# Integer shift adds on 64-bit words, norms' roots on ScalarE, and GpSimd's arithmetic moved to VectorE

## The chip, the cores and the metric

The kernel runs on one core of a Trainium2 chip. The metric is the device time of one execution in microseconds. Five engines work side by side, each with its own in-order queue: TensorE (PE, with its weight loads shown apart as PEld), VectorE (DVE), ScalarE (ACT), GpSimd (POOL) and SyncE (SP), which here only issues DMAs.

## The reference

Two layers, each an attention block A with one key and value head shared by 32 query heads, and a block B that mixes neighbouring rows and runs an MLP. Every block has a layer norm ahead of it, and B has two more inside. Sequence 2048, width 512, head width 16, bf16.

```python
def _A_ref(x, wq, wk, wv, wo):
    q = (x @ wq).reshape(B, S, H, Dh).transpose(0, 2, 1, 3)      # H = 32, Dh = 16
    k, v = x @ wk, x @ wv
    p = _softmax(jnp.einsum("bhqd,bkd->bhqk", q, k) * (Dh ** -0.5))
    o = jnp.einsum("bhqk,bkd->bhqd", p, v)
    return o.transpose(0, 2, 1, 3).reshape(B, S, H * Dh) @ wo
def _B_ref(x, w1, w2, w3, w4):
    h = _gelu(_layernorm(x) @ w1)
    ...                                  # four quarters of h shifted by 1, -1, 2, -2 rows
    x1 = x + hs @ w2
    return x1 + _gelu(_layernorm(x1) @ w3) @ w4        # w3: 512 x 1792
for _ in range(2):
    x = x + _A_ref(_layernorm(x), ...)
    x = x + _B_ref(_layernorm(x), ...)
```

The heavy part is the exponentials: 32 heads x 2048 x 2048 scores in each of two layers.

## The kernel before

A planner in the code (`Plan`) simulates the five engines with a duration for every operation, takes the ready operation with the lowest priority number on each engine, and so writes out a fixed order for each engine's queue, with semaphore waits between them. A table of rules (`MOODS`), chosen anew every 5 us of planned time by a string (`TEMPER`), steers its choices: how many fillers, how eagerly pairs are handed to VectorE, how many shift adds go to GpSimd. The order on the chip is therefore static; when an operation takes another time than planned, the queues wait but do not reorder.

Attention runs over the chunks of queries (four of 512 rows in layer 0; three of 512 and two of 256 in layer 1), in a chunk over 8 blocks of four heads, and in a block over the keys. Its work comes in *halves*: a 128 x 1024 piece of scores, two heads. The 2048 halves are shared out between two ways of taking the exponential.

- A *unit* (`declare_unit`): TensorE writes the scores to two PSUM banks, ScalarE's Exp takes both to EA in bf16 (L1240), TensorE multiplies with the values VP (L1352, four matmuls).
- A *pair* (`declare_pair`): VectorE casts a linear function of the scores to uint16 (L1260, two casts), so that the integer's bits, read as bf16, are a coarse exponential. Two more such rows follow by adding STEP = 43 to the integers, one after the other (`shift_op`, L1297, on GpSimd or VectorE; mostly two rows in one instruction, one of the second step and one of the first). TensorE multiplies all three with values that are weighted by three constants, VD (L1352, twelve matmuls), and their sum is the finer exponential. Five slots J hold pairs under way. `borrow` and `lent` move a waiting add between the two engines.

Beside the attention of one chunk, the planner places the side work of the chunk before it: the output projection, `mixer_in` (norm, norm of the norm, W1, Gelu), `mix` (W2 on shifted rows), `mlp` (norm, W3, Gelu, W4) and the next layer's norm and projections. The last chunk's side work has no attention beside it: the tail. Exp and Gelu are in different tables of ScalarE, so Gelus are bundled, with a table load before and behind.

A norm is `stats` on VectorE (L904, L906), `rstd` for the root, and `apply` on VectorE (L941). In `rstd`, GpSimd adds epsilon (L926, on VectorE at the start) and raises to the power -0.5 with the constant tile MH (L924). `mixer_in` needs the norm of a norm: three small operations more (L930 to L934), a second power, and the scaling of Y to ZR on GpSimd (L1627). In `mlp`, GpSimd also adds Y to X (L1723); in `scale_pair` it spreads reciprocals (L1452), and it copies edge columns of GP (L1673, L1675). A matmul filler (L790, ONES and NIL) keeps TensorE busy when the planner sees it idle.

Of the kernel before, what the change touches and what calls it, by code (L numbers as in the profile page):

```python
# [8 lines left out]
dt = mybir.dt  # L9
# [34 lines left out]
class Plan:  # L44
# [184 lines left out]
    def _pick(self, eng, t, dense=False):  # L229
# [20 lines left out]
        for o in h:  # L250
            if o.ready > t + 1e-9 or o.entry > t + self.EAGER:
                continue
            if eng == "ACT" and self.lock is not None and o.grp is not self.lock:
                continue
            if eng == "ACT" and self.closing and o.side and not all(u.placed for u in self.units[-4:]):
# [36 lines left out]
            best = (key, o)  # L292
            bank = k
# [333 lines left out]

def t_x2(n):
    return 0.066 + n * 0.522e-3
# [10 lines left out]
EPS = 1e-5  # L640
LOG2E = 1.4426950408889634


class Kernel:
# [21 lines left out]
    PORTION = 2  # L666
    QUICK = -1
# [32 lines left out]
        "40600c804b0c70477ac77e7194dc79a6b4c9e70863c1123547ccaa20177534ca0aa0dc405814470c4705413104"  # L700
        "7c1600071c825488640d166cc06053e94164c76c007310602612d80c0c1121b4db0561c3763ca8c50f5820c114"
        "076cc327266480d100a70d6e5394770058ec0700210e43c02c7a1a7307cb2ed6658250706076c138a756cb5e43"
        "813a0801110213220"
    )

    def __init__(self, nc, ins, out):
        self.stretch = -1
        self.nc = nc
        self.ins = ins
        self.out = out  # L710
        self.pl = Plan(nc, self.POOL_BANKS)
# [18 lines left out]
    def memory(self):  # L730
# [40 lines left out]
        self.MH = sb("MH", [2, 16], dt.float32)  # L771
# [52 lines left out]
    def head(self):  # L824
# [24 lines left out]
        fill("POOL", self.MH, -0.5, [("MH",)], 0.1, -8)  # L849
# [15 lines left out]
        def clear(ap, n, tags, prio):  # L865
            op("ACT", lambda e: e.memzero(ap), writes=tags, dur=0.1 + n / 2400, prio=prio)
# [5 lines left out]
        for c in range(4):  # L872
# [7 lines left out]
        fill("POOL", self.SELC, 0.0, [("SELC",)], 0.1, 3)  # L880
# [4 lines left out]
           reads=[("SELC",)], writes=[("SELC",)], dur=0.2, prio=3)  # L885
# [14 lines left out]

    def stats(self, src, tiles, tagf, prio):
# [7 lines left out]
    def rstd(self, tiles, prio, both=False):  # L909
# [3 lines left out]
        k = 2 if both else 1  # L913
        early = prio is not None
        prio = prio if early else self.QUICK
# [3 lines left out]
        var, aux = self.SM[:, 2, a:b], self.SM[:, 3, a:b]  # L919
        one, two = self.SM[:, 0, a:b], self.SM[:, 1, a:b]  # L920
        eng = "DVE" if early else "POOL"

        def power(out, src, tags, r):
            op("POOL", lambda e: e.tensor_tensor(out=out, in0=src, in1=self.MH[:, 0, a:b], op=ALU.pow),  # L924
               reads=tags + [("MH",)], writes=tg(r), dur=0.3 + 0.2 * (b - a), prio=prio)
        op(eng, lambda e: e.tensor_scalar(out=var, in0=mv, scalar1=EPS, scalar2=None, op0=ALU.add),  # L926
           reads=tg("MV"), writes=tg("S2"), dur=0.23 if eng == "POOL" else 0.08, prio=prio, port=True)
        power(one, var, tg("S2"), "R1")
        if both:
            op(eng, lambda e: e.tensor_tensor(out=aux, in0=one, in1=one, op=ALU.mult),  # L930
               reads=tg("R1"), writes=tg("S3"), dur=0.23 if eng == "POOL" else 0.08, prio=prio, port=True)
            op(eng, lambda e: e.tensor_tensor(out=aux, in0=aux, in1=mv, op=ALU.mult),
               reads=tg("MV"), writes=tg("S3"), dur=0.23 if eng == "POOL" else 0.08, prio=prio, port=True)
            op(eng, lambda e: e.tensor_scalar(out=aux, in0=aux, scalar1=EPS, scalar2=None, op0=ALU.add),  # L934
               writes=tg("S3"), dur=0.23 if eng == "POOL" else 0.08, prio=prio, port=True)
            power(two, aux, tg("S3"), "R2")


    def apply(self, out, src, tb, tags, writes, dur, prio):

        self.pl.op("DVE", lambda e: e.tensor_scalar(  # L941
            out=out, in0=src, scalar1=self.MV[:, tb, 0:1], scalar2=self.SM[:, 0, tb:tb + 1],
            op0=ALU.subtract, op1=ALU.mult),
            reads=tags + [("MV", tb), ("R1", tb)], writes=writes, dur=dur, prio=prio, port=True)
# [280 lines left out]
    def declare_unit(self, g):  # L1225
# [14 lines left out]
        o = q.feeds = op("ACT", lambda e: e.activation(self.EA[:, ea, :, :],  # L1240
# [52 lines left out]
    def shift_op(self, d, f, rows):  # L1293
# [3 lines left out]
        o = self.pl.op(eng, lambda e: e.tensor_scalar(  # L1297
            out=self.J[:, d, :], in0=self.J[:, f, :], scalar1=float(self.STEP), scalar2=1.0, op0=ALU.add, op1=ALU.mult),
            reads=[t for r in rows for t in self.jtag(r - 1)], writes=[t for r in rows for t in self.jtag(r)],
            dur=t_x4(1024 * n) if eng == "DVE" else 0.264 + 0.859 * n, prio=2, side=False, port=True,  # L1300
# [316 lines left out]
    def mixer_in(self, la, c, tiles, tail):  # L1617
# [4 lines left out]
        for part in self.portions(tiles):  # L1622
            self.stats(lambda tb: self.X[:, tb, :], part, lambda tb: ("X", tb), None)
            self.rstd(part, None, both=True)
            for tb in part:
                self.apply(self.Y[:, tb % 6, :], self.X[:, tb, :], tb, [("X", tb)], [("Y", tb % 6)], 0.33, None)
                op("POOL", lambda e, tb=tb: e.tensor_scalar(  # L1627
                    out=self.ZR[:, tb % 4, :], in0=self.Y[:, tb % 6, :], scalar1=self.SM[:, 1, tb:tb + 1],
                    scalar2=0.0, op0=ALU.mult, op1=ALU.add),
                   reads=[("Y", tb % 6), ("R2", tb)], writes=[("ZR", tb % 4)],  # L1630
                   dur=0.68, prio=self.QUICK, port=True)
# [5 lines left out]
        for f in range(4):  # L1637
# [10 lines left out]
            if tail:  # L1648
                op("ACT", lambda e, f=f, L=L: e.activation(self.GP[:, par, f, 2:2 + n],
# [10 lines left out]
        if not tail:  # L1660
            grp = Group()
            op("ACT", lambda e: e.activation(self.GP[:, par, :, 2:2 + n], self.GP[:, par, :, 2:2 + n],  # L1662
# [46 lines left out]
    def mlp(self, la, tiles, tail):  # L1709
# [12 lines left out]
        for tb in tiles:  # L1722
            op("POOL", lambda e, tb=tb: e.tensor_tensor(out=self.X[:, tb, :], in0=self.Y[:, tb % 6, :],  # L1723
                                                       in1=self.X[:, tb, :], op=ALU.add),
               reads=[("Y", tb % 6)], writes=[("X", tb)], dur=1.24, port=True)
        for f in range(14):
# [10 lines left out]
            if tail:  # L1737
                op("ACT", lambda e, f=f, L=L: e.activation(self.G2E[f][0][:, 0:n], self.PB[:, L.bank, 0:n],
# [14 lines left out]
    def gelus(self, tiles, joined=(), grp=None):  # L1753

        grp = grp or Group()
        for i in range(len(tiles)):
            self.pl.op("ACT", lambda e, i=i: e.activation(  # L1757
# [65 lines left out]
```

## Time and profile before

| | us |
|---|---|
| three runs, median (lowest to highest) | 1448.71 (1447.62 to 1449.34) |
| span of the profiled execution | 1444.3 |
| PE busy | 1418.6 (98%) |
| ACT busy | 1374.8 (95%) |
| DVE busy | 1321.9 (92%) |
| POOL busy | 1175.3 (81%) |

The span runs from the first to the last instruction of one profiled execution; the times of the runs also hold what lies around it, about 4.4 us at the median. Busy time is the union of an engine's instructions; consecutive ones overlap, so a group's mean is longer than its busy time over its count. Matmul ends are modelled, so a busy PE isn't PE at its peak. A row of the groups gives line, engine, operation, output and input with shapes, count, busy us, mean ns of one, and the idle time in front of them with what ended it.

### The profile page before, as it was taken

What the parts mean: (1) busy time and instruction counts of PE and PEld (TensorE: products, weight loads), DVE (VectorE), ACT (ScalarE), POOL (GpSimd) and SP (SyncE); (2) the same over time, 40 slices, a digit from 0 to 9 for tenths busy, and PEclk for the clock granted to TensorE, in tenths of its full rate; (3) what the DMA queues carried; (4) which work ended last, traced back from release to release, by engine and by line L of the source; (5) the groups of instructions that cost most, each with busy time, mean ns of one, the idle gap of its engine ahead of it and who ended that gap; (6) DMA issues with size and microseconds to landing.
All of it is one profiled execution on the core that took longest, in us unless ns stands there. A gap on an engine that the chain in (4) does not pass through costs nothing.

```text
span 1444.3 us, 65460 instructions
## 1 busy us (share of the span) xinstructions
PE 1418.6 (98%) x29768; PEld 637.7 (44%) x29768; DVE 1321.9 (92%) x2392; ACT 1374.8 (95%) x1463; POOL 1175.3 (81%) x846
## 2 busy tenths in 40 slices
PE   8999999999999999999999999999999999999999
PEld 4344334443444444444454444434434445545555
DVE  8999999999999999999988899999998999979863
ACT  7999999999999999999979999999999999999952
POOL 3888899998988978988855788998887988888841
DMA  6100100001000000010000000100000000000000
GB/s 221 31 5 6 21 6 6 5 6 20 6 5 7 6 7 4 7 21 3 2 3 3 3 11 9 21 6 5 6 12 17 6 6 14 8 17 12 7 14 25
DMA packets 32662, 21.76 MB, mean 15 GB/s; under 512 B 13056, under 2 KB 31872, under 8 KB 32384
## 3 DMA queue, kind: packets, MB, share of 16 engines
q1 hardware_dynamic: 32384, 17.57, 5.3%
q8 instruction: 233, 3.82, 1.1%
q14 instruction: 45, 0.37, 0.1%
HBM read 7.90 MB, written 2.10 MB: 7 GB/s over the span
## 4 chain that ended last, share of the span: by engine, by line
ACT 57%; PE 26%; DVE 8%; POOL 7%; issue 1%; DMA 0%; SPq 0%; POOLq 0%
ACT EA L1240 54%; PE PB L1197 8%; PE PB L1352 8%; PE PB L790 8%; POOL J L1297 6%; DVE J L1260 4%; ACT G L1757 2%; DVE J L1297 1%; PE PB L1121 1%; DVE ST L904 1%; PE PB L988 1%; POOL SM L924 1%; ACT L1240 1%; ACT GP L1662 1%; DVE G L1742 0%
## 5 line engine op out<-in xcount | busy, mean ns | idle before, releaser
L1240 ACT ACTIVATE EA<-PB 128x1024 bf16<-128x1024 f32 x1381 | 1272.0, 1149 | 11.3 <-PE PB L1197 10.6
L1297 POOL TENSOR_SCALAR J<-J 128x2048 uint16<-128x2048 uint16 (+1 forms) x550 | 1003.2, 1824 | 165.7 <-DVE J L1260 75.8
L1260 DVE TENSOR_SCALAR J<-PB 128x512 uint16<-128x512 f32 x1334 | 853.9, 680 | 49.9 <-PE PB L1197 44.5
L1197 PE MATMUL PB<-QT,KT 32*128 32x512 bf16 (+1 forms) x4608 | 586.5, 359 | 7.6 <-ACT EA L1240 3.1
L1352 PE MATMUL PB<-J,VD 128*32 128x256 bf16 (+1 forms) x8988 | 423.1, 264 | 6.5 <-DVE J L1297 1.4
L1352 PE MATMUL PB<-EA,VP 128*32 128x256 bf16 (+1 forms) x6220 | 351.9, 264 | 3.2 <-ACT EA L1240 1.8
L1197 PEld LDWEIGHTS PB<-QT,KT 32*128 32x128 bf16 x4608 | 159.6, 91 | 366.7 <-ACT EA L1240 277.8
L1352 PEld LDWEIGHTS PB<-J,VD 128*32 128x32 bf16 x8988 | 191.0, 95 | 154.4 <-issue 103.0
L1352 PEld LDWEIGHTS PB<-EA,VP 128*32 128x32 bf16 x6220 | 144.7, 95 | 142.0 <-issue 120.9
L790 PE MATMUL PB<-ZT,W 128*32 128x512 bf16 (+2 forms) x2816 | 169.5, 342 | 0.0
L1297 DVE TENSOR_SCALAR J<-J 128x2048 uint16<-128x2048 uint16 (+1 forms) x155 | 110.5, 713 | 13.0 <-POOL J L1297 10.9
L790 PE MATMUL PB<-W,G 128*32 128x512 bf16 x1624 | 105.6, 381 | 0.4 <-issue 0.4
L790 PEld LDWEIGHTS PB<-ZT,W 128*32 128x32 bf16 x2816 | 63.3, 96 | 34.4 <-issue 25.8
L1742 DVE CAST G<-PB 128x512 bf16<-128x512 f32 (+2 forms) x126 | 71.4, 577 | 4.7 <-PE PB L790 4.2
L924 POOL TENSOR_TENSOR SM<-SM,MH 128x2 f32<-128x2 f32 (+1 forms) x69 | 53.3, 774 | 21.8 <-DVE SM L926 13.3
L1757 ACT ACTIVATE G<-G 128x1792 bf16<-128x1792 bf16 x29 | 46.9, 1683 | 23.6 <-DVE G L1742 23.6
L790 PEld LDWEIGHTS PB<-W,G 128*32 128x32 bf16 x1624 | 36.8, 96 | 40.1 <-issue 15.3
L1723 POOL TENSOR_TENSOR X<-Y,X 128x512 bf16<-128x512 bf16 x32 | 39.4, 1242 | 12.2 <-DVE Y L1705 10.1
L904 DVE BATCH_NORM_STATS2 ST<-X 128x6 f32<-128x512 bf16 x64 | 42.8, 679 | 2.2 <-DMA X<-in_A_x_dram 1.8
L1392 DVE CAST ACCF<-PB 128x512 bf16<-128x512 f32 (+1 forms) x65 | 39.9, 614 | 0.8 <-PE PB L1352 0.7
L790 PE MATMUL PB<-WO,OT 128*32 128x512 bf16 x512 | 37.6, 381 | 0.0
L790 PE MATMUL PB<-W,GP 128*32 128x512 bf16 x512 | 34.2, 380 | 1.0 <-ACT GP L1662 1.0
(106 smaller groups left out, 706.2 us busy)
## 6 DMA issues: line engine op xcount, KB each, us to landing
OT<-ACCF SPq DMA_DIRECT2D x432, 8.0 KB, 1.8
W<-in_B_w_dram SPq DMA_DIRECT2D x2, 1792.0 KB, 13.9
X<-in_A_x_dram SPq DMA_DIRECT2D x8, 256.0 KB, 6.0
QT<-QS SPq DMA_DIRECT2D x32, 64.0 KB, 2.5
out_dram<-OUTB SPq DMA_DIRECT2D x16, 128.0 KB, 1.7
OT<-ACCF SPq DMA_DIRECT2D x112, 4.0 KB, 2.2
W<-in_B_w_dram SPq DMA_DIRECT2D x2, 512.0 KB, 8.6
WQ<-in_A_wq_dram SPq DMA_DIRECT2D x1, 512.0 KB, 5.5
```

The lines of the kernel that those rows point to most:

```text
L790: ins = e.matmul(self.PB[32 * g:32 * g + 32, bank, 0:n], lhsT=lhsT[:, 32 * g:32 * g + 32], rhs=rhs, start=start, stop=stop, tile_position= ...
L904: op("DVE", lambda e, tb=tb: e.bn_stats(self.ST6[:, tb, :], src(tb)), reads=[tagf(tb)], writes=[("ST", tb)], dur=0.606, prio=prio)
L924: op("POOL", lambda e: e.tensor_tensor(out=out, in0=src, in1=self.MH[:, 0, a:b], op=ALU.pow), reads=tags + [("MH",)], writes=tg(r), dur=0. ...
L1197: ins = e.matmul(self.PB[:, bank, j * n:(j + 1) * n], lhsT=self.KT[32 * h:32 * h + 32, la, (kb + j) * 128:(kb + j + 1) * 128], rhs=self.QT ...
L1240: o = q.feeds = op("ACT", lambda e: e.activation(self.EA[:, ea, :, :], self.PB[:, L.bank[0]:L.bank[0] + 2, :], ACTF.Exp, scale=0.25), writ ...
L1260: o = op("DVE", lambda e, i=i, L=L: e.tensor_scalar(out=self.J[:, 3 * s, i * 512:(i + 1) * 512], in0=self.PB[:, L.bank, :], scalar1=128 * ...
L1297: o = self.pl.op(eng, lambda e: e.tensor_scalar(out=self.J[:, d, :], in0=self.J[:, f, :], scalar1=float(self.STEP), scalar2=1.0, op0=ALU.a ...
L1352: ins = e.matmul(self.PB[32 * x:32 * x + 32, A.bank, p * hw:p * hw + hw], lhsT=v[:, la, kb + j, :], rhs=ap[:, i, j * w + u * hw:j * w + u ...
L1392: self.last_copy = op("DVE", lambda e: e.tensor_copy(acc, self.PB[:, A.bank, 0:n]), writes=[ac] + am, dur=t_ps(n), prio=0, side=False, give=A)
L1723: op("POOL", lambda e, tb=tb: e.tensor_tensor(out=self.X[:, tb, :], in0=self.Y[:, tb % 6, :], in1=self.X[:, tb, :], op=ALU.add), reads=[(" ...
L1742: op("DVE", lambda e, f=f, L=L: e.tensor_copy(self.G2[:, f, 0:n], self.PB[:, L.bank, 0:n]), writes=[L] + [(x, f, i) for x in ("G2", "GE") ...
L1757: self.pl.op("ACT", lambda e, i=i: e.activation(self.G2[:, :, i * 128:(i + 1) * 128], self.G2[:, :, i * 128:(i + 1) * 128], ACTF.Gelu_appr ...
```

## The change

- The shift adds on GpSimd become `int64_add`: the uint16 rows are viewed as 64-bit words, 256 a row, and the constant 0x002B002B002B002B is added to each. VectorE keeps its uint16 form. The planned time falls from 0.264 + 0.859 n to 0.25 + 0.44 n us for n rows.
- This operation lives in another library of GpSimd, which is loaded at the start, and the standard one is loaded again behind the last shift add. (At the start the code loads it ahead of the second of two fills of EPSB.)
- `rstd` runs on ScalarE: Ln with scale and a per-partition bias EPSB, then Exp with scale -0.5. The root of the norm of a norm comes straight from the variance, by Ln of v (1 + eps) + eps^2, so both roots need two Ln and one Exp. Only the tail's last norms (in `mlp`) stay on GpSimd, with its power.
- `table` pins the table: Exp of the scores, Ln and Exp of the norms come from one set, Gelus from another.
- GpSimd's scaling of Y to ZR becomes an `apply` on VectorE from X with the second root; the add of Y to X goes to VectorE except in the tail.
- A condition for ScalarE near the end lets side operations without a group and with negative priority pass; SELC is made earlier; `TEMPER` is another string.

```diff
@@ borrow/lent, durations
-        o.eng, o.dur, o.after = "POOL", 1.123 if o.flex < t_x4(1500) else 1.982, 0.07
+        o.eng, o.dur, o.after = "POOL", t_64(1 if o.flex < t_x4(1500) else 2), 0.07
...
+def t_64(n):
+    return 0.25 + 0.44 * n
@@ head
-        fill("POOL", self.MH, -0.5, [("MH",)], 0.1, -8)
+        for i, v in enumerate((EPS, EPS * EPS)):
+            fill("POOL", self.EPSB[:, i:i + 1], v, [("EPS",)], 0.1, -8)
...
+        self.library(library_config.all_libraries[1], [("ID",), ("SELC",)], [("HALF",)])
...
+    def library(self, lib, reads, writes):
+        def f(e):
+            e.load_library(lib)
+            return e.memset(self.HALF, -0.5)
+        self.pl.op("POOL", f, reads=reads, writes=writes, dur=8.0, prio=-5)
@@ rstd
+        for j in range(2 if both else 1):
+            op("ACT", lambda e, j=j: self.table(e).activation(
+                self.SM[:, 2 + j, a:b], mv, ACTF.Ln, scale=1.0 + j * EPS, bias=self.EPSB[:, j:j + 1]),
+               reads=tg("MV") + [("EPS",)], writes=tg(f"S{2 + j}"), dur=self.T_LN, prio=prio)
+        n = 2 if both else 1
+        op("ACT", lambda e: self.table(e).activation(self.SM[:, 0:n, a:b], self.SM[:, 2:2 + n, a:b], ACTF.Exp, scale=-0.5),
+           reads=tg("S2") + (tg("S3") if both else []), writes=tg("R1") + (tg("R2") if both else []),
+           dur=self.T_EXP, prio=prio)
+    def table(self, e, name="natural_log_exp_and_others"):
+        if self.loaded != name:
+            e.preload_act_table_set(name)
+            self.loaded = name
+        return e
@@ shift_op
+        words = self.J.rearrange("p r c -> p (r c)").bitcast(dt.uint64)
+        words = self.shaped(words, [3 * self.N_J, 256])
+        def add(e):
+            if hasattr(e, "int64_add"):
+                return e.int64_add(words[:, d, :], words[:, f, :], self.STEP * 0x0001000100010001)
+            return e.tensor_scalar(out=self.J[:, d, :], in0=self.J[:, f, :], scalar1=float(self.STEP), scalar2=1.0,
+                                   op0=ALU.add, op1=ALU.mult)
...
-            dur=t_x4(1024 * n) if eng == "DVE" else 0.264 + 0.859 * n, prio=2, side=False, port=True,
+            dur=t_x4(1024 * n) if eng == "DVE" else t_64(n), prio=2, side=False, port=True,
@@ chunk_end
+        if tail:
+            self.library(library_config.standard, [t for r in range(3 * self.N_J) for t in self.jtag(r)], [("HALF",)])
@@ mixer_in
-                op("POOL", lambda e, tb=tb: e.tensor_scalar(
-                    out=self.ZR[:, tb % 4, :], in0=self.Y[:, tb % 6, :], scalar1=self.SM[:, 1, tb:tb + 1],
-                    scalar2=0.0, op0=ALU.mult, op1=ALU.add),
...
+                self.apply(self.ZR[:, tb % 4, :], self.X[:, tb, :], tb, [("X", tb)], [("ZR", tb % 4)], 0.33, None, 1)
@@ mlp
-            self.rstd(part, None)
+            self.rstd(part, None, pool=tail)
...
-            op("POOL", lambda e, tb=tb: e.tensor_tensor(out=self.X[:, tb, :], in0=self.Y[:, tb % 6, :],
-                                                       in1=self.X[:, tb, :], op=ALU.add),
-               reads=[("Y", tb % 6)], writes=[("X", tb)], dur=1.24, port=True)
+            op("POOL" if tail else "DVE", lambda e, tb=tb: e.tensor_tensor(
+                out=self.X[:, tb, :], in0=self.Y[:, tb % 6, :], in1=self.X[:, tb, :], op=ALU.add),
+               reads=[("Y", tb % 6)], writes=[("X", tb)], dur=1.24 if tail else 0.335, port=True)
```

More of the change, by code (lines that the diff above doesn't have):

```diff
@@ L6 @@
 import concourse.bass as bass
-from concourse import mybir
+from concourse import library_config, mybir
 dt = mybir.dt
@@ L254, in _pick @@
                 continue
-            if eng == "ACT" and self.closing and o.side and not all(u.placed for u in self.units[-4:]):
+            if eng == "ACT" and self.closing and o.side and (o.grp is not None or o.prio >= 0) \
+                    and not all(u.placed for u in self.units[-4:]):
                 continue
@@ L666 @@
     PORTION = 2
+    T_LN = 0.16
+    T_EXP = 0.07
     QUICK = -1
@@ L865, in clear @@
         def clear(ap, n, tags, prio):
[L866 removed]
+            op("ACT", lambda e: self.table(e).memzero(ap), writes=tags, dur=0.1 + n / 2400, prio=prio)
         clear(self.VD, 3072, vd, -7)
@@ L879, in head @@
         self.qproj(0, 0, prio=3, blocks=range(2, 8), after=[("KT", 0, 7)])
-        fill("POOL", self.SELC, 0.0, [("SELC",)], 0.1, 3)
+        fill("POOL", self.SELC, 0.0, [("SELC",)], 0.1, -8.5)
         fill("POOL", self.RZ, 0.0, [("RZ", b) for b in range(8)], 0.1, 3)
@@ L912, in rstd @@
         mv = self.MV[:, a:b, 1]
-        k = 2 if both else 1
-        early = prio is not None
-        prio = prio if early else self.QUICK
+        prio = self.QUICK if prio is None else prio
         def tg(name):
             return [(name, t) for t in tiles]
[L919 to L936, printed above, removed]
@@ L939, in apply @@
-    def apply(self, out, src, tb, tags, writes, dur, prio):
+        if pool:
+            var, one = self.SM[:, 2, a:b], self.SM[:, 0, a:b]
+            op("POOL", lambda e: e.tensor_scalar(out=var, in0=mv, scalar1=EPS, scalar2=None, op0=ALU.add),
+               reads=tg("MV"), writes=tg("S2"), dur=0.23, prio=prio, port=True)
+            op("POOL", lambda e: e.tensor_tensor(out=one, in0=var, in1=self.HALF[:, 0:b - a], op=ALU.pow),
+               reads=tg("S2") + [("HALF",)], writes=tg("R1"), dur=0.3 + 0.2 * (b - a), prio=prio)
+            return
@@ L941, in apply @@
+    def table(self, e, name="natural_log_exp_and_others"):
[3 more added lines that the diff above has]
+        return e
+    def apply(self, out, src, tb, tags, writes, dur, prio, k=0):
         self.pl.op("DVE", lambda e: e.tensor_scalar(
-            out=out, in0=src, scalar1=self.MV[:, tb, 0:1], scalar2=self.SM[:, 0, tb:tb + 1],
+            out=out, in0=src, scalar1=self.MV[:, tb, 0:1], scalar2=self.SM[:, k, tb:tb + 1],
             op0=ALU.subtract, op1=ALU.mult),
-            reads=tags + [("MV", tb), ("R1", tb)], writes=writes, dur=dur, prio=prio, port=True)
+            reads=tags + [("MV", tb), (f"R{1 + k}", tb)], writes=writes, dur=dur, prio=prio, port=True)
@@ L1239, in declare_unit @@
         q = op("PE", fpe, reads=self.inputs(g), writes=[L], pe=("Q", 512, 256, hs), prio=0, side=False, take=L)
-        o = q.feeds = op("ACT", lambda e: e.activation(self.EA[:, ea, :, :],
+        o = q.feeds = op("ACT", lambda e: self.table(e).activation(self.EA[:, ea, :, :],
                                                        self.PB[:, L.bank[0]:L.bank[0] + 2, :],
@@ L1648, in mixer_in @@
             if tail:
-                op("ACT", lambda e, f=f, L=L: e.activation(self.GP[:, par, f, 2:2 + n],
+                op("ACT", lambda e, f=f, L=L: self.table(e, GELU).activation(self.GP[:, par, f, 2:2 + n],
                                                            self.PB[:, L.bank, 0:n], ACTF.Gelu_apprx_tanh),
@@ L1661, in mixer_in @@
             grp = Group()
-            op("ACT", lambda e: e.activation(self.GP[:, par, :, 2:2 + n], self.GP[:, par, :, 2:2 + n],
+            op("ACT", lambda e: self.table(e, GELU).activation(self.GP[:, par, :, 2:2 + n], self.GP[:, par, :, 2:2 + n],
                                              ACTF.Gelu_apprx_tanh),
@@ L1737, in mlp @@
             if tail:
-                op("ACT", lambda e, f=f, L=L: e.activation(self.G2E[f][0][:, 0:n], self.PB[:, L.bank, 0:n],
+                op("ACT", lambda e, f=f, L=L: self.table(e, GELU).activation(self.G2E[f][0][:, 0:n], self.PB[:, L.bank, 0:n],
                                                            ACTF.Gelu_apprx_tanh),
@@ L1756, in gelus @@
         for i in range(len(tiles)):
-            self.pl.op("ACT", lambda e, i=i: e.activation(
+            self.pl.op("ACT", lambda e, i=i: self.table(e, GELU).activation(
                 self.G2[:, :, i * 128:(i + 1) * 128], self.G2[:, :, i * 128:(i + 1) * 128], ACTF.Gelu_apprx_tanh),
```

22 lines of the change are left out of this document (11 added, 11 removed).

## The prediction

> **What bounds the kernel now.** I read the windows of busy time first, then the chain that ended last, then the groups by line and form. The windows below are cut where the chain changes hands (columns: window, its length, busy us and instruction count of PE, PEld, DVE, ACT, POOL, then the granted clock).
>
> ```profile
> span 1444.3 us, 65460 instructions
> ...
> 0.00:36.00 36.00, 32.23 (x682) 15.01 (x682) 31.28 (x96) 25.70 (x26) 11.12 (x29) 1.00 0.68 222
> 36.00:695.00 659.00, 650.78 (x12296) 274.12 (x12298) 628.93 (x1090) 656.32 (x704) 581.76 (x381) 1.00 0.05 9
> 695.00:765.00 70.00, 69.53 (x1475) 34.03 (x1467) 62.15 (x127) 59.43 (x56) 44.27 (x49) 1.00 0.01 3
> 765.00:1205.00 440.00, 433.93 (x8442) 187.37 (x8439) 411.83 (x724) 439.24 (x470) 375.55 (x251) 1.00 0.04 9
> 1205.00:1388.00 183.00, 178.68 (x5632) 95.00 (x5632) 163.06 (x304) 176.50 (x186) 150.23 (x115) 1.00 0.06 11
> 1388.00:1444.30 56.30, 53.49 (x1264) 32.22 (x1264) 24.65 (x55) 17.58 (x25) 12.42 (x23) 1.00 0.08 24
> ```
> ```profile
> 561.08 1.28 ACT L1240
> 562.37 0.01 issue
> 562.38 131.19 ACT EA L1240 x143
> 693.57 0.02 issue
> ...
> 1387.96 9.90 PE PB L790 x180
> ...
> PEld PB L1197 <- ACT EA L1240: 277.8, 937, 0.6
> ```
>
> In 36 to 695 and 765 to 1205, ACT is idle for 2.7 and 0.8 us of 1099: the chain runs through unbroken rows of exponentials, one every 131.19/143 = 0.917 us. PE looks as full, but its weight loads spend 277.8 us waiting for ACT to free a bank, so PE follows. In 1205 to 1388 ACT has 6.5 us to spare and the chain is in PE; the last 56 us are the last block's matmuls. The clock is 1.00 throughout. So a microsecond taken off ACT is worth a microsecond in 1099 of the 1444, and little in the rest.
>
> **The change, part by part.** The groups by form (busy us, mean ns of one):
>
> ```profile
> L1240 ACT ACTIVATE EA<-PB 128x1024 bf16<-128x1024 f32 x1381 | 1272.0, 1149 | 11.3 <-PE PB L1197 10.6
> L1297 POOL TENSOR_SCALAR J<-J 128x2048 uint16<-128x2048 uint16 x495 | 941.4, 1902 | 144.5 <-DVE J L1260 59.8 <-DVE J L1297 52.2 <-DVE MV L906 0.9
> L1260 DVE TENSOR_SCALAR J<-PB 128x512 uint16<-128x512 f32 x1334 | 853.9, 680 | 49.9 <-PE PB L1197 44.5
> L1297 DVE TENSOR_SCALAR J<-J 128x2048 uint16<-128x2048 uint16 x134 | 98.4, 734 | 12.9 <-POOL J L1297 10.9
> L1297 POOL TENSOR_SCALAR J<-J 128x1024 uint16<-128x1024 uint16 x55 | 61.8, 1124 | 21.1 <-DVE J L1260 16.0 <-DVE J L1297 1.5 <-POOL J L1297 0.2
> L924 POOL TENSOR_TENSOR SM<-SM,MH 128x2 f32<-128x2 f32 x59 | 47.5, 806 | 21.2 <-DVE SM L926 13.3 <-DVE MV L906 5.1
> L1723 POOL TENSOR_TENSOR X<-Y,X 128x512 bf16<-128x512 bf16 x32 | 39.4, 1242 | 12.2 <-DVE Y L1705 10.1 <-DVE J L1260 1.3 <-DVE X L1613 0.2
> L1627 POOL TENSOR_SCALAR ZR<-Y,SM 128x512 bf16<-128x512 bf16 x32 | 23.3, 736 | 2.1 <-DVE Y L941 0.4 <-DVE RZ L1416 0.3 <-DVE J L1260 0.2
> L790 PE MATMUL PB<-ONES,NIL 128*32 128x512 bf16 x248 | 22.6, 428 | 2.7 <-DVE WQ L843 1.7 <-DVE ST L904 0.5 <-DVE ZT L997 0.3
> L941 DVE TENSOR_SCALAR Y<-X,MV,SM 128x512 bf16<-128x512 bf16 x32 | 12.1, 418 | 1.1 <-POOL SM L924 0.9
> L1297 DVE TENSOR_SCALAR J<-J 128x1024 uint16<-128x1024 uint16 x21 | 12.1, 576 | 0.1
> L1613 DVE TENSOR_TENSOR X<-PB,X 128x512 bf16<-128x512 f32 x32 | 21.6, 678 | 1.6 <-PE PB L790 1.6
> ```
>
> *Shift adds on 64-bit words (POOL).* Counted in the two built programs, POOL's adds go from 495 of two rows and 55 of one to 641 and 81, and DVE keeps 19 and 11 of its 134 and 21. No row shows a 64-bit add. From the two POOL forms an add costs 1902 - 1124 = 778 ns per 1024 elements and 346 ns fixed. Lower end: the fixed part alone, 0.35 us. Upper end: as now, 1.90. I take 1.12, the 1024-element row, since two rows are 512 words, or 1024 halves of 32 bits, if each half costs what an element costs; one row then 0.73. POOL's work becomes 641 x 1.12 + 81 x 0.73 = 777 us, and about 45 for what stays, against 1175: off the path, it costs nothing while below some 1.8 us an add (rival 3).
>
> *DVE.* Casts of further pairs: +78 x 853.9/1334 = +49.9. Shift adds: -(98.4 + 12.1) + 19 x 0.73 + 11 x 0.58 = -90. ZR's scaling moves here, 32 at 12.1/32 = 0.38, +12; the X adds, 29 between 0.38 and 21.6/32 = 0.68 (PSUM form): +11 to +20, I take +15. Sum -13 of 1322: DVE stays just under ACT, and that room is what buys the 78 casts. Since it hides behind ACT it counts nothing itself.
>
> *Exponentials moved off ACT.* The programs hold 1381 and 1342 of them: 39 fewer, each 0.917 us of a full ACT: **-35.8 us**.
>
> *The norms' roots on ACT.* 118 small activations come: 67 Ln and 51 Exp, 21 of them at the start or in the tail, where ACT waits anyway, 97 in the stream. No row is that small. The nearest:
>
> ```profile
> L1649 ACT ACTIVATE GP<-PB 128x256 bf16<-128x256 f32 x4 | 1.5, 384 | 7.5 <-PE PB L790 7.4
> ...
> L1738 ACT ACTIVATE EA<-PB 128x384 bf16<-128x384 f32 x14 | 6.0, 490 | 2.5 <-PE PB L790 2.4
> ...
> 554.62 6.44 ACT L1757 ACTIVATE G<-G 128x1792 bf16<-128x1792 bf16 x4
> ```
>
> The first two differ by 106 ns for 128 elements, 0.83 ns each. So an exponential in the row carries 917 - 848 = 69 ns beyond its elements (lower end), and an activation from SBUF 6440/4 - 1484 = 126 ns. Upper end: 384 - 212 = 172 ns alone, and the overlap 1149 - 917 = 232 lost beside it, 0.40 us. I take 126, the SBUF row, as Ln and Exp read SBUF: 97 x 0.126 = **+12.2** (ends +6.7 and +39). In the program an exponential of the scores stands between nearly every Ln and the Exp that needs it, so the wait of Exp is covered.
> [...]
> Table loads stay 22, as Ln and Exp are taken from one set. Two of them now stand in the tail, before and behind the last norms, 1.28 us each by the row at 561.08, and ACT waits 7.4 us there (the row of L1649): nothing. [...]
>
> *Start.* POOL loads another library ahead of its second fill of the two constants, and the first Ln waits for that fill; behind that Ln stand in ACT's queue the copies that open the first chunk and all exponentials. DVE's program now puts three more pairs of stats, up to those of the second load of X, ahead of the first ZR.
>
> ```profile
> 1.66 0.19 POOL L882 TENSOR_SCALAR_AFFINE_SELECT SELC<-SELC 128x4 bf16<-128x4 bf16 x1
> ...
> 6.24 1.52 POOL L924 TENSOR_TENSOR SM<-SM,MH 128x2 f32<-128x2 f32 x2 [1.85 <-DVE MV L906]
> ...
> 6.99 1.54 DVE L941 TENSOR_SCALAR ZR<-X,MV,SM 128x512 bf16<-128x512 bf16 x4 [0.48 <-POOL SM L924]
> 9.05 1.29 DVE L904 BATCH_NORM_STATS2 ST<-X 128x6 f32<-128x512 bf16 x2 [0.52 <-DMA X<-in_A_x_dram]
> ...
> 15.05 7.44 ACT L1240 ACTIVATE EA<-PB 128x1024 bf16<-128x1024 f32 x8 [1.52 <-PE PB L1197]
> ...
> 1379.20 1.90 POOL L1297 TENSOR_SCALAR J<-J 128x2048 uint16<-128x2048 uint16 x1 [0.81 <-DVE J L1297]
> 1388.60 0.19 POOL L1673 COPY GP<-GP 128x8 bf16<-128x8 bf16 x1 [7.50 <-ACT GP L1662]
> ```
>
> Before, the first ZR starts at 6.99; now not before the second load's stats, 9.05 + 2 x 0.65 = 10.4 and more, 3.5 to 4 us later, but that stats work is then done. I take **+3** (ends 0 and +4), if the library is there by 10 us: the planner in the code puts it at 8.0 us, from about 1.9. Every microsecond beyond adds one. No row shows a load. [...]
>
> *Tail.* A second load, of the first library, stands behind the last shift add; behind it wait the copies into GP and the last roots, which stay on POOL. The last add ends at about 1381 now and the GP copies come at 1388.6 (7.5 us idle), so a load of 8 us costs at most one; Ln, Exp and DVE's ZR save about one against POOL's chain of six. Nothing.
>
> *PE.* 39 pairs have 8 more matmuls of 256 columns each; at 9.90/180 x 4 = 0.22 us for 512 columns on four column groups that is 39 x 0.22 = +8.6, and 88 filler matmuls fewer are -4.8: +3.8 in all, covered by the waits for ACT. In 1205 to 1388, where PE leads, ACT loses 6 exponentials and PE's steps hardly change: about 5.5 of the gain is not had there, and some 2 to 3 us of Ln and Exp there are hidden: **+3**.
>
> Sum: -35.8 + 12.2 + 3 + 3 = -17.6; the span 1444.3 becomes 1426.7. The three runs have a median of 1448.71, 4.4 over the span: 1431.1. DVE's and POOL's operations on one port should wait for each other a little less, which no row prices; I round down to **1430**.
>
> **The rivals.**
>
> 1. *Ln and Exp cost ACT more than the exponentials saved* (slower). Place: ACT between 36 and 1205. For: one waits on DVE in an in-order queue that had no gap, and Exp waits on Ln. It decides from (35.8 - 6)/97 = 0.31 us each; at the upper end, 0.40, the time is 1448.7 - 35.8 + 39 + 6 = 1458. Against: the SBUF row at 126 ns and the exponentials set between them.
> 2. *PE takes over as the bound.* For: busy 98%, the chain in PE from 1205. Against: 277.8 us of its loads wait for ACT. The gain is lost and the +3.8 shows: about 1450 (1446 to 1453).
> 3. *The 64-bit adds are no cheaper than the old ones.* At 1.90 POOL has 641 x 1.90 + 81 x 1.12 + 45 = 1354 us to do between 31 and 1381, in an order written out for less: POOL leads, and waits come on top: 1450 to 1465. The same place is reached by a library load of 25 us or more at the start.
> 4. *More is won*: small activations at 69 ns, nothing lost at the start or under PE: 1448.7 - 35.8 + 6.7 = 1420; fewer port waits between POOL and DVE could add some us: 1412 to 1423.
>
> **How the numbers follow.** Forecast (1423 to 1437) 0.52; rival 4, 0.16; a smaller gain, from mixed upper ends (1437 to 1445.8), 0.12; rival 1, 0.07; rival 2, 0.06; rival 3, 0.07. What a measurement here can tell from no change is 0.2%, 2.9 us (1445.8 to 1451.6); of rivals 1 to 3 about 0.04 fall there. So faster 0.80, same 0.04, slower 0.16. The range, 1417 to 1450, leaves out the lower half of rival 4 and most of rivals 1 and 3; 1423 to 1437 is the forecast's own.
>
> **What would show it.** Right: 1342 exponentials at about 0.92 us in unbroken rows; Ln and Exp with a busy time under 20 us in all and no idle row of ACT put down to DVE's MV; POOL near 820 us with two-row adds at 1.1 us; the first ZR near 10.5 us and the first exponential about 3 us later than its 15.05; the chain still mostly in ACT. Wrong: idle time of ACT behind Ln; two-row adds near 1.9 us; a first Ln well past 10 us; PE's waits for ACT gone.

## The result, and the profile after

The changed kernel takes 1423.6 us (median of four runs, 1422.62 to 1424.24) where the kernel before took 1449.03 beside it: a ratio of 0.9826, 95% interval 0.9812 to 0.9840. It is 25.4 us faster; 18.7 were forecast. The page of the changed kernel, its span, busy times and chain:

```profile
span 1421.7 us, 66135 instructions
...
PE 1401.5 (99%) x30008; PEld 641.6 (45%) x30008; DVE 1299.4 (91%) x2398; ACT 1354.0 (95%) x1542; POOL 748.0 (53%) x802
...
ACT 56%; PE 39%; DVE 4%; issue 1%; DMA 0%; POOL 0%; SPq 0%; DVEq 0%
```

POOL fell from 81% of the span to 53%. ACT, at 95% as before, has 20.8 us less to do (1374.8 to 1354.0), and the span is 22.6 us shorter: nearly all of the gain is ACT's. The other 2.8 of the 25.4 lie in the choice of the execution that was profiled. In the runs of the changed kernel span and time differ by 2.0 to 2.1 us each time, and for the kernel before, in the runs beside the experiments, by 1.8 to 2.1. So the profiled execution with its span of 1444.3 took an estimated 1446.4, some 2.3 less than the median of its kernel, and the 4.4 us are not what lies around a span.

Where ACT waits is told by the windows, cut at about the same points of the work: the start of the unbroken rows of exponentials, the two stretches in which the chain had been in PE, and the end of the last exponential. First the kernel before (columns as in the prediction; ACT's busy time is the fourth after the length), then the changed one.

```profile
0.00:34.80 34.80, 31.03 (x660) 14.47 (x664) 30.49 (x92) 24.50 (x24) 9.99 (x29) 1.00 0.70 230
34.80:695.00 660.20, 651.99 (x12320) 274.65 (x12320) 629.72 (x1094) 657.52 (x705) 582.89 (x382) 1.00 0.05 9
...
1205.00:1383.00 178.00, 173.88 (x5504) 92.57 (x5504) 158.98 (x296) 174.74 (x185) 150.23 (x115) 1.00 0.06 12
1383.00:1444.30 61.30, 58.29 (x1392) 34.65 (x1384) 28.73 (x64) 19.34 (x26) 12.42 (x23) 1.00 0.07 22
```
```profile
0.00:36.30 36.30, 32.52 (x663) 14.59 (x663) 30.57 (x85) 25.43 (x39) 2.88 (x22) 1.00 0.67 220
36.30:680.00 643.70, 638.60 (x12462) 277.04 (x12465) 619.05 (x1104) 642.34 (x725) 384.50 (x391) 1.00 0.05 10
680.00:745.00 65.00, 64.82 (x1382) 31.63 (x1378) 55.60 (x120) 55.52 (x70) 14.70 (x17) 1.00 0.01 3
745.00:1190.00 445.00, 441.57 (x8864) 194.91 (x8856) 416.14 (x745) 444.52 (x499) 252.69 (x265) 1.00 0.04 9
1190.00:1358.00 168.00, 163.57 (x5276) 87.69 (x5262) 146.92 (x279) 163.50 (x182) 87.46 (x96) 1.00 0.06 12
1358.00:1421.70 63.70, 60.45 (x1402) 35.73 (x1401) 31.07 (x69) 22.70 (x34) 5.78 (x12) 1.00 0.07 21
```

ACT's idle time, length less busy: start 10.3 to 10.9; the two full stretches 2.7 + 0.8 to 1.4 + 0.5; the two with PE in the chain 10.6 + 3.3 to 9.5 + 4.5; tail 42.0 to 41.0. In sum -1.8 us. So -20.8 of work and -1.8 of waiting make up the -22.6.

The groups by form of the changed kernel (busy us, mean ns of one | idle before):

```profile
L1262 ACT ACTIVATE EA<-PB 128x1024 bf16<-128x1024 f32 x1342 | 1244.8, 1187 | 8.8 <-PE PB L1219 8.6
L1324 POOL INT64_ADD J<-J x722 | 718.6, 996 | 590.9 <-DVE J L1282 507.7 <-DVE MV L925 25.0 <-DVE VD L1096 13.1
L945 ACT ACTIVATE SM<-MV,EPSB 128x2 f32<-128x2 f32 x58 | 18.6, 389 | 3.3 <-POOL EPSB L853 2.2 <-DVE MV L925 0.9
L949 ACT ACTIVATE SM<-SM 128x2 f32<-128x2 f32 x26 | 6.7, 260 | 0.1
L1750 DVE TENSOR_TENSOR X<-Y,X 128x512 bf16<-128x512 bf16 x29 | 12.4, 432 | 0.0
```

And the roots of a norm of a norm in ACT's order of time (start, us, what), which gives their price from start to start:

```profile
195.60 0.61 ACT L945 ACTIVATE SM<-MV,EPSB 128x2 f32<-128x2 f32 x2
195.98 1.16 ACT L1262 ACTIVATE EA<-PB 128x1024 bf16<-128x1024 f32 x1
196.88 0.34 ACT L949 ACTIVATE SM<-SM 128x4 f32<-128x4 f32 x1
196.98 9.41 ACT L1262 ACTIVATE EA<-PB 128x1024 bf16<-128x1024 f32 x10
```

Two Ln hold ACT for 0.38 us and Exp for 0.10, though the rows show 389 ns for one Ln and 0.34 us for this Exp: the rest overlaps the instructions beside them.

### The profile page after: what moved, and what is told of

The parts are those of the page before. It is cut to its first block, busy times and chain, and to the rows that moved or that the text cites. A ratio compares the mean times of both kernels' runs of the same rounds, so it can differ in the third digit from the quotient of the medians.

```text
span 1421.7 us, 66135 instructions
## 1 busy us (share of the span) xinstructions
PE 1401.5 (99%) x30008; PEld 641.6 (45%) x30008; DVE 1299.4 (91%) x2398; ACT 1354.0 (95%) x1542; POOL 748.0 (53%) x802
## 4 chain that ended last, share of the span: by engine, by line
ACT 56%; PE 39%; DVE 4%; issue 1%; DMA 0%; POOL 0%; SPq 0%; DVEq 0%
ACT EA L1262 53%; PE PB L1381 13%; PE PB L800 12%; PE PB L1219 12%; DVE J L1282 1%; ACT L956 1%; DVE ST L923 1%; PE PB L1010 1%; ACT G L1784 1%; DVE G L1769 0%; ACT SM L945 0%; DMA X<-in_A_x_dram 0%; DVE Y L1732 0%; DVE ZR L963 0%; ACT GP L1689 0%
## 5 line engine op out<-in xcount | busy, mean ns | idle before, releaser
L1262 ACT ACTIVATE EA<-PB 128x1024 bf16<-128x1024 f32 x1342 | 1244.8, 1187 | 8.8 <-PE PB L1219 8.6
L1324 POOL INT64_ADD J<-J x722 | 718.6, 996 | 590.9 <-DVE J L1282 507.7
L1282 DVE TENSOR_SCALAR J<-PB 128x512 uint16<-128x512 f32 x1412 | 901.7, 683 | 49.3 <-PE PB L1219 44.2
L1219 PE MATMUL PB<-QT,KT 32*128 32x512 bf16 (+1 forms) x4608 | 571.0, 359 | 5.3 <-ACT EA L1262 2.9
L1381 PE MATMUL PB<-J,VD 128*32 128x256 bf16 (+1 forms) x9480 | 440.3, 264 | 2.8 <-issue 0.8
L1381 PE MATMUL PB<-EA,VP 128*32 128x256 bf16 (+1 forms) x6056 | 344.2, 264 | 2.0 <-issue 1.1
L1219 PEld LDWEIGHTS PB<-QT,KT 32*128 32x128 bf16 x4608 | 155.3, 91 | 361.9 <-ACT EA L1262 286.9
L1381 PEld LDWEIGHTS PB<-J,VD 128*32 128x32 bf16 x9480 | 206.2, 95 | 143.5 <-issue 115.3
L1809 DVE TENSOR_TENSOR OUTB<-PB,X 128x512 bf16<-128x512 f32 x16 | 11.0, 689 | 25.9 <-PE PB L800 25.8
L1010 PE MATMUL PB<-IDENT,ZR 128*32 128x128 bf16 x1328 | 29.0, 220 | 0.8 <-issue 0.5
```

The lines of the kernel that those rows point to most:

```text
L1010: ins = e.transpose(self.PBH[32 * g:32 * g + 32, L.bank, x:x + 128], rows[:, tb % 4, y:y + 32], self.IDENT, tile_position=(0, 32 * g))
L1219: ins = e.matmul(self.PB[:, bank, j * n:(j + 1) * n], lhsT=self.KT[32 * h:32 * h + 32, la, (kb + j) * 128:(kb + j + 1) * 128], rhs=self.QT ...
L1262: o = q.feeds = op("ACT", lambda e: self.table(e).activation(self.EA[:, ea, :, :], self.PB[:, L.bank[0]:L.bank[0] + 2, :], ACTF.Exp, scale ...
L1282: o = op("DVE", lambda e, i=i, L=L: e.tensor_scalar(out=self.J[:, 3 * s, i * 512:(i + 1) * 512], in0=self.PB[:, L.bank, :], scalar1=128 * ...
L1324: return e.int64_add(words[:, d, :], words[:, f, :], self.STEP * 0x0001000100010001)
L1381: ins = e.matmul(self.PB[32 * x:32 * x + 32, A.bank, p * hw:p * hw + hw], lhsT=v[:, la, kb + j, :], rhs=ap[:, i, j * w + u * hw:j * w + u ...
```

## The experiments

The changed kernel's ratio to the kernel before, 0.9826, is the mark for the runs below; each has its own ratio to the kernel before on its chip. The first four keep the changed kernel's order on every engine and alter what one engine has to do.

**ACT: the roots twice.**

```diff
-            op("ACT", lambda e, j=j: self.table(e).activation(self.SM[:, 2 + j, a:b], mv, ACTF.Ln, ...),
+            op("ACT", lambda e, j=j: [self.table(e).activation(o, mv, ACTF.Ln, ...)
+                for o in (self.pad(b - a), self.SM[:, 2 + j, a:b])][1],
 ...                                        # Exp likewise
```

> Changed kernel, same order on every engine; each of the 67 Ln and 51 Exp of the norms is issued a second time, into a scratch tile. Theory (ACT bounds, and a small activation costs what its start-to-start time in the trace is, 0.19 us for Ln and 0.09 for Exp): ACT gets 67 x 0.19 + 51 x 0.09 = 17 us more, about 14 of it in the full stretch, and the time goes from 1423.6 to about 1438. Rival (ACT has room, the norms' roots are hidden): 1423 to 1427. Rival (a small activation breaks the overlap, 0.40 us): 1460.

Measured: ratio 0.9938 (0.9923 to 0.9953), 1.1% or 16 us over the mark; ACT's busy time went from 1354.0 to 1369.7. Each microsecond put on ACT came out in the time. The second set of roots cost some 16 us, as their start-to-start times had it, and nothing near the 0.40 us each of the second rival.

**TensorE: less to do.**

```diff
+            if part == 2:
+                return e.matmul(self.PB[0:32, A.bank, p * hw:p * hw + 32], lhsT=v[:, la, kb, :], rhs=ap[:, 0, 0:32], ...)
```

> Changed kernel, same order; the third product of every pair is cut to one matmul of 32 columns, so the third row's share of the output is left out and TensorE has 706 x 4 matmuls of 256 columns, some 75 us of work, less. Theory (TensorE follows ACT except between 680 and 745 and 1190 and 1358 us): 3 to 10 us faster than 1423.6. Rival (TensorE is the bound): 50 us or more faster.

Measured: 0.9790 (0.9775 to 0.9804), 5 us under the mark for some 75 us of matmuls. Of those, only 32.5 us show in PE's busy time (1401.5 to 1369.0); matmul ends are modelled, so that figure is rough. From the page of this run:

```profile
PE 1369.0 (97%) x27554; PEld 606.1 (43%) x27554; DVE 1297.3 (92%) x2398; ACT 1351.1 (96%) x1542; POOL 746.3 (53%) x802
...
ACT 86%; PE 9%; DVE 3%; DMA 0%; issue 0%; POOL 0%; SPq 0%; DVEq 0%
```

PE's share of the chain falls from 39% to 9% and the time hardly moves: PE isn't the bound, although it is 99% busy in the changed kernel.

**VectorE: less to do.**

```diff
-                out=self.X[:, tb, :], in0=self.Y[:, tb % 6, :], in1=self.X[:, tb, :], op=ALU.add),
+                out=self.X[:, tb, 0:16], in0=self.Y[:, tb % 6, 0:16], in1=self.X[:, tb, 0:16], op=ALU.add),   # not in the tail
 ...                                        # the scaling to ZR with the second root likewise
```

> Changed kernel, same order; the 32 scalings to ZR with the second root and the 29 adds of Y to X that came to VectorE work on 16 columns in place of 512, so most of the normed rows and of the sums are left out, and VectorE has about 61 x 0.33 = 20 us less to do. Theory (VectorE hides behind ACT, the move cost nothing): 0 to 4 us faster than 1423.6. Rival (VectorE bounds, the moved arithmetic cost its full time): 15 to 20 us faster.

Measured: 0.9830 (0.9815 to 0.9845), no gain. VectorE lost 10 us of work, not 20 (1299.4 to 1289.4): a scaling of 16 columns still takes 319 ns and an add 172, where 512 columns took some 430. By the rival 10 us should have come out; none did. The moved arithmetic is hidden behind ACT.

**GpSimd: slower adds.** The constant is read from a tile in place of the instruction, which makes a two-row add 1.89 us (median) instead of 1.04.

```diff
-                return e.int64_add(words[:, d, :], words[:, f, :], self.STEP * 0x0001000100010001)
+                return e.int64_add(words[:, d, :], words[:, f, :], self.C43.bitcast(dt.uint64))
```

> Changed kernel, same order; GpSimd's 64-bit add takes its constant from a one-word-per-partition tile in place of the instruction, which should make it longer by some tenths of a microsecond; nothing else differs but one small fill. Theory (GpSimd is off the path up to some 1.8 us for a two-row add): within 5 us of 1423.6 if the two-row add stays below 1.8. Rival (the add's latency holds the pairs, so the gain came from the shorter add itself): over 15 us slower for half a microsecond an add.

Measured: 1.2045 (1.2006 to 1.2083), some 320 us over the mark. At 1.89 us the add lies just beyond the 1.8 of the theory, but a loss of this size is far from what it let expect. Two runs followed with every second and every fourth add slow, so that the mean stays below 1.8:

> Changed kernel, same order; every second 64-bit add on GpSimd has the slow form of the run before (1.89 us for two rows in place of 1.04), a mean of 1.47; GpSimd's work grows by about 290 us to some 1040, 73% of the span. With all adds slow the time was 1.2045 of the kernel before. Theory now (what counts is not GpSimd's share but that a pair's two dependent adds hold its slot and TensorE's fixed order longer than planned): already well over the changed kernel's 0.983, about a third of the loss, near 1.05. Rival (capacity: GpSimd has room up to a mean of some 1.8 us): 0.983 to 0.990.

> As above with every fourth add slow, a mean of 1.25 us and GpSimd near 890 us. Theory (slots and fixed order): some loss, 0.990 to 1.01. Rival (capacity): 0.983 to 0.985.

Measured: 1.0551 (1.0530 to 1.0571) and 1.0110 (1.0095 to 1.0125). Against the mark, 145 us more of POOL work (748 to 893) cost 41 us, 289 cost 105, and 580 cost 320: 0.28, 0.36 and 0.55 us for each one, with POOL still 39, 32 and 24% idle. Capacity isn't what counts. The 320 us may not be the late adds alone: in that run the granted clock was 0.919 and a matmul of the scores took 417 ns in place of 384, where the other two have their profiled runs at 0.997 and 0.998. VectorE's busy time grew as well, by 12, 27 and 64 us from the fewest slow adds to the most; no run separates either from the lateness. The waits of the changed kernel, and of the run with all adds slow (who waits for whom: us in total, times, longest), show the ring:

```profile
PEld PB L1381 <- POOL J L1324: 13.1, 51, 0.8
ACT EA L1262 <- PE PB L1219: 8.6, 19, 1.5
```
```profile
PEld PB L1383 <- POOL J L1326: 261.9, 331, 1.8
ACT EA L1264 <- PE PB L1221: 256.5, 380, 3.2
POOL J L1326 <- DVE J L1284: 244.1, 173, 25.5
DVE J L1284 <- PE PB L1221: 233.2, 356, 3.7
```

PE, in its fixed order, waits for a late row of J; the scores behind it come late, and so ACT and DVE wait for PE, and POOL for DVE's casts. All four stand idle in turn. Already with a quarter of the adds slow, ACT's waits for the scores rise from 8.6 to 30.6 us. In all three runs the order was written for adds of 1.13 us. No run had it written anew for the slow ones, so how much of the loss a fitting order would save isn't shown.

**Code and table apart.** The planner's rule table was exchanged between the two kernels, and the 64-bit adds were taken out of the changed one. In all four runs neither code nor table is matched to the other, so they are compared among themselves.

```diff
 # old table: the changed kernel                # new table: the kernel before
-    TEMPER = ("098c4877...")                   -    TEMPER = ("40600c80...")
+    TEMPER = ("40600c80...")                   +    TEMPER = ("098c4877...")
 # no 64-bit adds: the changed kernel, GpSimd's adds in uint16 at 0.264 + 0.859 n, no library
-                return e.int64_add(...)
-            e.load_library(lib)
```

> The changed kernel with the rule table of before, so that neither code nor table is matched to the other: the programs hold 1396 exponentials (1342 with its own table) and 520 fillers. Theory (ACT's ledger: each exponential 0.917 us): 1421 + 54 x 0.917 = 1471 on this chip. Rival (the table hardly matters): 1421 to 1430. Compared with the kernel before under the new table: the code alone gains about 15 us by the ledger; rival (the gain lies in the table): no difference between the two.

> The kernel before with the rule table of the changed one, again unmatched: 1422 exponentials (1381 with its own). Theory (ledger): 1446.5 + 41 x 0.917 = 1484. Rival (the new table is better in itself): at or below 1446.

> The changed kernel, its new table, but GpSimd's adds as the uint16 adds of before, planned at their old price, and no library loaded: norms' roots on ACT and the moved arithmetic alone. Unmatched with its table: 1428 exponentials. Theory (ledger): 1421 + 86 x 0.917 = 1500, about 15 us slower than the kernel before under the unmatched table and 29 slower than the changed one under the unmatched table, so that the 64-bit adds carry all of the gain and the rest costs. Rival (the freed GpSimd and the shorter norms gain by themselves): below the unmatched kernel before, 1484.

> As the run without 64-bit adds, under the table of before: 1425 exponentials, 1497 by the ledger. It differs from its twin only in an unmatched table, and so shows how much the choice among unmatched tables moves the time: within 10 us if the comparison of unmatched kernels means something; more than 20 us if it does not.

| code under an unmatched table | exponentials | median us | ratio to the kernel before |
|---|---|---|---|
| kernel before | 1422 | 1527.6 | 1.0563 (1.0548 to 1.0579) |
| changed, without 64-bit adds, new table | 1428 | 1535.0 | 1.0614 (1.0596 to 1.0631) |
| the same, old table | 1425 | 1535.6 | 1.0615 (1.0599 to 1.0632) |
| changed | 1396 | 1495.2 | 1.0339 (1.0323 to 1.0354) |

Between the two kernels, code alone, the change is worth 32 us here (1527.6 to 1495.2), where 15 were expected. All four are 24 to 44 us slower than expected. The count of exponentials is only part of it, as the busy lines of the kernel before under the new table, and of the changed one under the old, show:

```profile
span 1528.2 us, 65587 instructions
...
PE 1488.7 (97%) x29916; PEld 652.5 (43%) x29916; DVE 1314.4 (86%) x2307; ACT 1410.7 (92%) x1502; POOL 1095.8 (72%) x801
```
```profile
span 1493.5 us, 65765 instructions
...
PE 1453.8 (97%) x29896; PEld 650.5 (44%) x29896; DVE 1268.8 (85%) x2306; ACT 1403.3 (94%) x1596; POOL 673.3 (45%) x718
```

ACT's busy time grew as counted (+36 for 41 exponentials, +49 for 54), but its idle time went from 69.5 to 117.5 and from 67.7 to 90.2: the one other table that was tried costs 5 to 6% on either code. Among unmatched kernels the norms on ACT and the moved arithmetic alone are 0.5% *slower* than the kernel before (1.0614 to 1.0563; expected about 15 us, measured 7), and the 64-bit adds bring 2.6% (1.0614 to 1.0339; expected 29 us, measured 40). So the 64-bit adds carry the whole gain here, and the rival, that the freed GpSimd and the shorter norms gain by themselves, fell. The twins differ by 0.01%, so which unmatched table is used matters little for that code; that a matched table would give the same split isn't shown.

**The start.**

```diff
-            fill("POOL", self.EPSB[:, i:i + 1], v, [("EPS",)], 0.1, -8)
+            fill("POOL", self.EPSB[:, i:i + 1], v, [("EPS", i)], 0.1, -9)     # and the load behind the fills of VP and VD
```

> Changed kernel with the two fills of EPSB ahead of the library load and the load behind the other fills of the start; the planner then writes another order, so the table is unmatched (1390 exponentials, 456 fillers; the changed kernel under the table of before has 1396 and 520). Theory (the start cost 3 us because the first Ln waited for the load and the stats were put ahead of the first ZR): first ZR near 7 us in place of 10.8, first exponential near 15 in place of 18.6. The whole time is to be compared with the unmatched 1495 only: 1480 to 1492. Rival (the start is set by the landing of X's second load, whatever the norms do): first exponential still after 18 us.

The changed kernel's start in order of time, then this run's:

```profile
8.71 0.09 POOL L917 MEMSET HALF<- 128x2 f32 x1 [6.79 <-issue]
...
8.87 0.48 ACT L945 ACTIVATE SM<-MV,EPSB 128x2 f32<-128x2 f32 x2 [2.20 <-POOL EPSB L853]
...
10.84 1.37 DVE L963 TENSOR_SCALAR ZR<-X,MV,SM 128x512 bf16<-128x512 bf16 x4
...
18.61 2.85 ACT L1262 ACTIVATE EA<-PB 128x1024 bf16<-128x1024 f32 x3 [0.37 <-PE PB L1219]
```
```profile
7.12 1.39 DVE L963 TENSOR_SCALAR ZR<-X,MV,SM 128x512 bf16<-128x512 bf16 x4 [0.92 <-ACT SM L949]
...
15.38 3.77 ACT L1262 ACTIVATE EA<-PB 128x1024 bf16<-128x1024 f32 x4 [1.80 <-PE PB L1219]
```

The first ZR is back at 7.1 us and the first exponential at 15.4 in place of 18.6, as the theory had it. The whole time, 1498.8 (ratio 1.0345, 1.0318 to 1.0372), is not below the unmatched 1495.2: outside what was expected, so what the earlier start is worth in the end stays open.

**A scalar bias for Ln.**

```diff
-                ... ACTF.Ln, scale=1.0 + j * EPS, bias=self.EPSB[:, j:j + 1]),
+                ... ACTF.Ln, scale=1.0 + j * EPS, bias=(EPS, EPS * EPS)[j]),
```

> Changed kernel, same order; the bias of the 67 Ln is a scalar in the instruction in place of a one-word-per-partition tile, so the operand is the only thing that changes. [...] In the changed kernel's trace Ln takes 0.19 us from its start to the next and Exp 0.10, 0.09 apart. Theory (ACT bounds, and Ln's surplus is its pointer): some 54 Ln in the full stretch are 0.09 us shorter, 5 us in all, and the ratio to the kernel before goes from 0.9826 to 0.979 or 0.980. Rival (Ln's surplus is its own, or it is hidden): Ln still at 0.19 us, ratio 0.982 to 0.983.

The group of Ln:

```profile
L945 ACT ACTIVATE SM<-MV 128x2 f32<-128x2 f32 x58 | 12.8, 282 | 3.1 <-POOL EPSB L853 2.4 <-DVE MV L925 0.6
```

Ln went from 389 to 282 ns, from its start to the next from 0.19 to 0.10 us, and ACT's busy time from 1354.0 to 1349.0. So the surplus is the operand's, the tile that the expectation calls a pointer: 91 ns from start to start, and 107 between the means. The median is 1419.4, the ratio 0.9819 (0.9805 to 0.9832): the sign is the expected one, but the interval holds the mark of 0.9826, so a gain in time isn't shown.

## Why the prediction was right

- **The bound.** Right: ACT. Work added there came out whole (16 us), work taken from PE brought 5 us for 75 us of matmuls (32.5 of PE's busy time), and work taken from VectorE nothing. That the chain gives PE 39% and the page 99% would have misled.
- **The exponentials, -35.8.** Right, and a little more came. Summed in the traces from each start to ACT's next start, or to its own end where ACT then waits, they fell from 1272.0 to 1233.2 us, by 38.8. The 3.0 beyond 39 x 0.917 are some 2 ns for each of the 1342; what shortened them isn't shown. In the unbroken rows the step is still 0.916 us:

```profile
414.16 97.12 ACT EA L1262 x106
```

- **The roots, +12.2.** The count was right and the price low. Between 36.3 and 1358 us stand 97 roots, as forecast. Summed in the same way they hold ACT for 14.6 us, 0.15 each: 56 Ln at 0.19 and 41 Exp at 0.10. The 0.126 of the SBUF row is neither price; that it lies between them is luck. It took the 0.09 us that the bias in a tile adds to each Ln at nothing, and the run with a scalar bias shows it.
- **Start, +3.** About right. The first exponential was 3.6 us late (18.6, was 15.05) and the first ZR came at 10.84, as forecast. The unbroken rows begin at 36.3 us, were 34.8, with one exponential fewer ahead of them (17, were 18) and 1.9 us less of their work: 3.4 us in all. In ACT's books 3.1 of these stand as 16 roots and only 0.6 as idle time.
- **PE's stretch, +3.** This term is what failed. In the stretches where the chain is in PE, ACT's idle time is the same 14 us, so nothing of the gain was lost there. ACT was idle for only 3.3 of 178 us in the later one, and the chain's share had been read as a bound.
- **Tail and table loads, nothing.** Right in sum, by two errors. Three of the 22 loads stand behind the last exponential, where one stood before, which takes 2.6 us out of the stream. And from the last exponential to the end the kernel takes 2.4 us longer (63.7, was 61.3), though ACT's idle time fell by 1.0 there. PE leads the chain in the tail of both; what made it longer wasn't tested.
- **The sum for the span.** Forecast: -35.8 + 12.2 + 3 + 3 = -17.6. Measured: -38.8 of exponentials, +14.6 of roots in the stream, +3.4 at the start, +2.4 in the tail, -2.6 of table loads and -1.5 of ACT's idle time between start and tail, which is -22.5 against -22.6 for the span.
- **From span to time, +4.4.** Wrong by 2.5: for the changed kernel it is 1.9 between the profiled span and the median. With the 5.0 us by which the span was missed, less the 1.1 rounded off, this makes the distance of 6.4 us between 1430 and 1423.6. The measured time lies only 0.6 us inside the forecast's own range of 1423 to 1437; without the roots' error, which went the other way, it would have been further from 1430. The 1.1 were taken off for waits between DVE's and POOL's operations. No row prices them, but the traces show such waits: before, 38 of DVE's 251 shift adds and applies last over 0.15 us longer than the median of their form, 17.1 us in all, and each of the 38 ends behind an operation of POOL by the same 0.15 us (applies), 0.28 (one-row adds) or 0.55 (two-row adds); after, it is 8 of 187, with the X adds, and 3.6 us. That they are for one port isn't shown, nor that having fewer of them shortened the time, as DVE hides behind ACT.
- **The shift adds.** The two-row add measured 1.04 us and the one-row 0.61, where 1.12 and 0.73 were taken from the uint16 rows. "Off the path, it costs nothing while below some 1.8 us an add" was wrong, and with it the price of rival 3: at 1.89 the changed kernel's order takes 1740 us, not 1450 to 1465. In the changed kernel the adds came in slightly under the planned 1.13, so nothing of this was felt. The working compared POOL's total with the span; the runs with slow adds say that each add had to be compared with its planned time.
- **VectorE.** Hidden, as forecast. Its work fell by 22.5 us where 13 were forecast. The X adds came at 0.43 us (0.38 to 0.68 taken), and the `apply` from Y to ZR in `mlp`, which the change leaves as it was, went from 565 to 414 ns.
- **The signs.** Met: 1342 exponentials, the first ZR and the first exponential, the two-row adds and the chain in ACT. POOL was busy for 748 us, not 820. Ln and Exp hold ACT for 18.6 us from start to start, but their rows add up to 35.9, where under 20 was set, and 0.9 us of ACT's idle time ahead of Ln is put down to DVE's MV, where none was expected.
- **The other rivals.** Roots dearer than the exponentials saved: no, 0.15 against 0.31. PE taking over: no, by the run with less PE work. More to win, 1412 to 1423: missed by 0.6 us; of its premises, nothing was lost under PE, but the start lost its 3 us and the roots cost twice its 69 ns.

Not foreseen at all: that the matched table, against the one other that was tried on each code, is worth about three times the change itself (5.2 and 5.6% against 1.7%).

## What to carry to other kernels

Keep the books on the engine that hardly waits: count what it gains and loses in start-to-start times, with its work at the start and in the tail, and charge a delay elsewhere only where its idle time shows it. A share of busy time, or of the chain, doesn't make an engine the bound, and an idle share doesn't make it free: in this order, fixed beforehand, adds of 1.89 us where 1.13 were planned stalled all queues in turn even with their own engine idle for 24 to 39% of the time. When two versions are compared whose schedules were tuned, compare them untuned as well, or part of the schedule's gain goes to the edit.

## What the runs showed of the hardware that was not expected

- The library load shows as a gap and no row: 6.79 us ahead of the first operation behind it (8.71 in the fence on the start), and 7.23 us at the way back in the tail.
- The same 64-bit add is 1.04 us with its constant in the instruction and 1.89 with the constant in a tile, one word a partition.
- GpSimd's copy to RZE (128 x 512), which the change doesn't touch, went from 865 to 616 ns in the mean of 34. Before, 16 of them take 0.60 to 0.61 us; the other 18 (0.97 to 1.14) start while a shift add of VectorE is under way, and each ends 0.47 us behind that add. After, 33 take 0.61; the one of 0.80 starts in an add of Y to X and ends 0.47 us behind it. So the mean went with VectorE's adds, of which 155 became 30, and not with the library: a copy that meets no add takes the same before and after. The means of the other runs agree: 614 to 621 in three with 64-bit adds, 746 to 790 in the three without.
- In the run with all adds slow, the granted clock of TensorE was 0.919, with PE busy for 89% of the span; with every second add slow it was 0.997 at 93%, and in the changed kernel 1.00 at 99%. What lowers it isn't shown.
